# Attention, Fourier mixing and a feed-forward block on one core: a third batch turned on TensorE, another first chunk, a run-in of zeros and a new early order

## The chip, the core and the metric

The kernel runs on one core of one Trainium2 chip. The metric is device time in microseconds of one launch; lower is better. Engines are named as in the profile: PE (TensorE's products), PEld (its weight loads), DVE (VectorE), ACT (ScalarE), POOL (GpSimd), SP (the queue that issues most DMAs).

## The reference

```python
def _attn_ref(q, k, v):                     # B, H, S, D = 8, 8, 576, 64
    scores = scale * np.matmul(q, k.transpose(0, 1, 3, 2))
    # heads 0..3: the last 32 positions; heads 4..7: every 4th of the last 128
    scores = np.where(masks[None, :, :, :], scores, -1000000000.0)
    ...
    return np.matmul(attn, v)

def _moe_ref(x, w_ch1, w_ch2):              # x: [8, 576, 512]
    X = np.fft.fft(np.fft.fft(x, axis=1), axis=2)
    u = x + np.real(X).astype(np.float32)
    un = (u - mu) / np.sqrt(var + 1e-06)    # over the 512 channels
    ch = np.maximum(un @ w_ch1, 0.0) @ w_ch2   # 512 -> 2048 -> 512
    return u + ch
```

All of it is float32 in and out. Windowed attention makes x, the real part of a two-dimensional Fourier transform is added to it, and a feed-forward block with a residual follows.

## The kernel before, in words

**Two parts.** In the early part each of the eight batches goes through attention (`attend`), the Fourier mixing as products with cosine and sine tables (`mix`), and `normalise`, which writes the normalised rows to scratch memory (`us`, four tiles of 128 rows to a "chunk" of 512 tokens; eight chunks are the batches, the ninth holds the rows that are left over). Six of the sixteen blocks of hidden units are done right there (`fill`: `up` on line 1351, `down` on line 1368), as soon as a pair of tiles is there with the channels on the partitions. The other ten blocks are done in the late part, for one chunk after the other, in pairs of blocks by a scheme with seven products in place of eight (`two_tiles`, `product` on line 1746, `down7` on line 1856). The late part's operand, `xb`, is made by `load_blocks` from the chunk's turned tokens: sums and differences on line 1566, and high and low halves on lines 1576 (ACT) and 1579 (DVE). Float32 products are made of three fast ones, with a high and a low half of each operand.

**Turning tokens.** `normalise` leaves rows with the tokens on the partitions; both parts need the channels there. For the first two batches (`b < NPE`) `turned` does it on PE: four transposes per tile (line 975) into one of two PSUM banks named "mix", an ACT copy (line 981) for the high half and a DVE subtraction (line 982) for the low half. Mixing takes its banks from the same two. For the other batches `tokens` fetches the rows from `us` in four pieces (line 1489), DVE transposes blocks (line 1499), the turned tokens are stored in scratch memory for the late part (line 1522, `kept_t`, named tt in the profile), and ACT and DVE make the halves (lines 1528 and 1531). In the late part `load_blocks(c)` reads `kept_t` where it is there (two reads of 512 KB); for chunks 0 and 1 it fetches and transposes afresh.

**The order.** No order is written by hand: `Plan.run` places every operation in advance, on each engine the ready one with the lowest priority first, by costs and delays written into the planner. `MOVED` adds to the priorities, group by group (x: tables, k: keys and queries, v: values, s, p, o: steps of attention, l, f, q, e, c: steps of mixing, n: normalise, t: turning, u, d: feed-forward, w, W: weight loads and their conversion, and others), `HELD` adds to the earliest times. The engines run the resulting lists strictly in order. The weights come as 64-bit floats, and DVE and ACT convert them (lines 1254 to 1272 and 1307 to 1335); those of the late part that have no seat yet are written to scratch memory (line 1339, wt<-wst) and read again (line 1342). `keep_warm` issues a few products without use (line 1381) ahead of the late part.

**The join.** `load_blocks` for the first chunk and the weights' conversion share DVE, ACT and the DMA queues with the last `fill`s. The first chunk's four tiles get their buffers at once; later ones wait for a mark (`marks`).

**The start.** Batch 0's first scores (line 821, sixteen products of 64x64 per part) wait for q and k from memory. The first 32 columns of each k buffer are cleared by DVE (line 702).

Of the kernel before, what the change touches and what calls it, by code (L numbers as in the profile page):

```python
# [20 lines left out]
P = 128  # L21
# [22 lines left out]
LB_AT, PR_AT = 0, 0  # L44
# [13 lines left out]
NPE = 2  # L58
N_WARM0, N_WARM1 = 6, 5
NXT = 0  # L60
# [77 lines left out]
}  # L138
HELD = {
# [21 lines left out]
BURST, COST_SC, COST_AV = 0.25, 0.07, 0.07  # L161
NCH = B * S // TOK
NREST = 4 * B
NTILE = B * S // P
QG = 32
KG = 64
NG = 18
# [419 lines left out]
def fused_kernel(ctx: ExitStack, tc, q, k, v, w1, w2, seq, tail, rest32, chn, alt, mask, ident, flip, out):  # L587
# [1316 lines left out]
    for c in range(NCH):  # L1904
        if c:
            load_blocks(c, gate2, soon(P_LB))
# [48 lines left out]
```

## Time and profile before

| | us |
|---|---|
| median of 3 runs | 1023.43 (1023.1 to 1027.09) |
| the profiled execution | 1018.65 |
| its span, first to last instruction | 1016.9 |

| engine | busy us | share of the span |
|---|---|---|
| PE | 958.6 | 94% |
| DVE | 825.5 | 81% |
| ACT | 564.8 | 56% |
| POOL | 210.2 | 21% |

A span is the time from the first to the last instruction. Busy time is a union of instruction times; the end of a product on PE is modelled, and products overlap, so that PE at 94% isn't PE at its peak. PEclk is the granted clock of TensorE as a share of 2.4 GHz, DMA the mean busy share of the core's sixteen DMA engines. A wait is put down to what released it last.

### The profile page before, as it was taken

To read this page: it belongs to the slowest core of one execution; us is meant where nothing else is said; L and a number is where in the kernel's file an instruction comes from. 1 tells how busy PE (TensorE), PEld (TensorE's weight loads), DVE (VectorE), ACT (ScalarE), POOL (GpSimd) and SP (SyncE) were. 2 spreads that over 40 slices of the span, in tenths; PEclk is the share of its full clock that TensorE was granted. 3 is DMA by queue.
4 is the path that set the end of the run, shared out by engine and by line. 5 is a ranking of instruction groups with operands and counts; after the bars stand their busy time and mean duration, and the time that the engine had idled before them with its cause. 6 is when DMAs were issued, how large, how long until landed. Compare 5 with 4: busy or idle time off the path is not lost.

```text
span 1016.9 us, 29244 instructions
## 1 busy us (share of the span) xinstructions
PE 958.6 (94%) x11109; PEld 873.7 (86%) x11109; DVE 825.5 (81%) x2738; ACT 564.8 (56%) x1483; POOL 210.2 (21%) x277
## 2 busy tenths in 40 slices
PE   3499999999999999999998999999999999999997
PEld 2247788888878888998987999999999999999997
DVE  3799876777877798669888599888888888888887
ACT  2566646454555443236454575757575756575663
POOL 2301442635445446400003000000000000100011
PEclk9999999999999999999999999999999999999999
DMA  8767866878785554265798943131313131313031
GB/s 284 243 230 221 261 208 205 248 225 255 246 247 156 182 160 129 83 214 170 261 347 315 309 135 105 63 106 61 114 53 115 54 114 53 116 53 121 6 112 56
DMA packets 111510, 168.74 MB, mean 166 GB/s; under 512 B 13156, under 2 KB 53140, under 8 KB 111370
## 3 DMA queue, kind: packets, MB, share of 16 engines
q1 hardware_dynamic: 107452, 159.52, 49.8%
q0 software_dynamic: 2880, 6.43, 2.1%
q8 instruction: 88, 1.44, 0.6%
q10 hardware_dynamic: 1038, 0.92, 0.3%
q14 instruction: 52, 0.43, 0.1%
HBM read 111.47 MB, written 54.45 MB: 163 GB/s over the span
## 4 chain that ended last, share of the span: by engine, by line
PE 59%; DVE 9%; DMA 7%; issue 2%; ACT 1%; SPq 1%; POOL 1%; DVEq 0%; ACTq 0%; POOLq 0%
PE ff L1746 19%; PE ff L1351 6%; PE ff L1368 6%; PE mix L1856 6%; PE sc L1856 6%; PE sd L1856 5%; DMA ut<-us 3%; PE ff L1856 3%; PE mix L1163 2%; DMA wt<-wst 1%; PE sd L1351 1%; PE mix L1098 1%; DVE ut L1499 1%; DMA wst<-in_w_dram 1%; PE sc L1368 1%
## 5 line engine op out<-in xcount | busy, mean ns | idle before, releaser
L1421 POOL DMA_INDIRECT ut<-us,flip_sb x20 | 30.6, 1529 | 509.3 <-DVE ut L1450 158.3
L1351 PE MATMUL ff<-ut,wa 128*128 128x256 f32 x936 | 131.7, 287 | 3.6 <-DVE h L1360 1.9
L1351 PEld LDWEIGHTS ff<-ut,wa 128*128 128x128 f32 x936 | 117.4, 188 | 9.9 <-DVE h L1360 3.0
L1368 PE MATMUL ff<-wa,h 128*128 128x512 f32 x468 | 120.8, 400 | 0.7 <-DVE h L1360 0.7
L837 ACT ACTIVATE pm<-pm,mx 128x64 f32<-128x64 f32 x288 | 79.5, 339 | 68.1 <-DVE mx L831 56.4
L1368 PEld LDWEIGHTS ff<-wa,h 128*128 128x128 f32 x468 | 83.3, 188 | 17.6 <-DVE h L1360 0.9
L1746 PE MATMUL ff<-xb,wa 128*128 128x256 f32 x540 | 75.8, 281 | 0.1
L1746 PE MATMUL ff<-xb,left_w 128*128 128x256 f32 x486 | 69.2, 281 | 0.1
L1746 PEld LDWEIGHTS ff<-xb,wa 128*128 128x128 f32 x540 | 68.4, 188 | 0.3 <-ACT ut L1754 0.3
L1746 PE MATMUL ff<-xb,late_w 128*128 128x256 f32 x486 | 68.7, 280 | 0.0
L1770 ACT ACTIVATE h<-s 128x256 fp32r<-128x256 f32 x134 | 55.4, 417 | 19.3 <-DVE s L1786 14.5
L1746 PEld LDWEIGHTS ff<-xb,left_w 128*128 128x128 f32 x486 | 62.2, 188 | 0.5 <-ACT s L1754 0.3
L1746 PEld LDWEIGHTS ff<-xb,late_w 128*128 128x128 f32 x486 | 61.9, 188 | 0.1
L1746 PE MATMUL ff<-xb,right_w 128*128 128x256 f32 x378 | 55.0, 286 | 4.3 <-DVE xb L1579 2.7
L1746 PEld LDWEIGHTS ff<-xb,right_w 128*128 128x128 f32 x378 | 49.5, 193 | 5.4 <-DVE xb L1579 2.9
L1754 ACT COPY s<-ff 128x256 f32<-128x256 f32 x90 | 33.5, 372 | 33.4 <-PE ff L1746 32.5
L1358 ACT ACTIVATE h<-ff 128x256 fp32r<-128x256 f32 x78 | 28.5, 381 | 38.6 <-PE ff L1351 38.1
L1351 PEld LDWEIGHTS sd<-ut,wa 128*128 128x128 f32 x360 | 45.1, 188 | 3.5 <-DVE h L1360 2.2
L1351 PE MATMUL sd<-ut,wa 128*128 128x256 f32 x360 | 46.5, 281 | 0.5 <-DVE h L1360 0.4
L1499 DVE STREAM_TRANSPOSE ut<-ut 128x512 f32<-128x512 f32 (+1 forms) x40 | 38.9, 996 | 8.9 <-DMA ut<-us 5.1
L1360 DVE SCALAR_TENSOR_TENSOR h<-ff,h 128x256 fp32r<-128x256 f32 x78 | 31.6, 418 | 17.3 <-ACT h L1358 16.9
L1368 PE MATMUL sc<-wa,h 128*128 128x512 f32 x180 | 44.2, 391 | 0.0
(309 smaller groups left out, 2629.0 us busy)
## 6 DMA issues: line engine op xcount, KB each, us to landing
vt<-in_v_dram SPq DMA_DIRECT2D x64, 260.0 KB
wst<-in_w_dram SPq DMA_DIRECT2D x20, 512.0 KB
wt<-wst SPq DMA_DIRECT2D x40, 256.0 KB
us<-uc SPq DMA_DIRECT2D x36, 257.0 KB
part<-row SPq DMA_DIRECT2D x36, 256.0 KB
ut<-part SPq DMA_DIRECT2D x36, 256.0 KB
kb<-in_k_dram SPq DMA_DIRECT2D x30, 288.0 KB
ut<-us SPq DMA_DIRECT2D x56, 128.0 KB
```

The lines of the kernel that those rows point to most:

```text
L837: add("ACT", 0.25, lambda i=i: nc.scalar.activation(out=pm()[:, i], in_=pm()[:, i], func=AF.Exp, bias=mx()[:, i:i + 1], scale=-1.0), ((mx, ...
L1163: nc.tensor.matmul(ps()[:n, :NEP], lhsT=ys[i]()[:, dt, a, rows], rhs=chn_sb[i]()[:, dt, c], start=(dt == 0 and x == 0), stop=(i == 1 and d ...
L1351: nc.tensor.matmul(z()[:, :n_tok], lhsT=wf()[:, a, kk], rhs=ut()[:, p, kk], start=(kk == 0 and n == 0), stop=(kk == KT - 1 and n == 2),)
L1358: add("ACT", act(n_tok) - 0.03, lambda: nc.scalar.activation(out=h()[:, 0, :n_tok], in_=z()[:, :n_tok], func=AF.Relu), (z,), ((h, 0),), prio)
L1360: add("DVE", dve(n_tok), lambda: nc.vector.scalar_tensor_tensor(h()[:, 1, :n_tok], z()[:, :n_tok], 0.0, h()[:, 0, :n_tok].bitcast(F32), op ...
L1368: nc.tensor.matmul(acc(), lhsT=h()[:, a, P * s:P * s + P], rhs=wf()[:, p], start=(first and n == 0), stop=(last and n == 2),)
L1421: add("POOL", 1.3, lambda: nc.gpsimd.indirect_dma_start(u(0, C + 2), None, us[idx // 4](), bass.IndirectOffsetOnAxis(ap=flip_sb()[:, 4 * k ...
L1499: nc.vector.transpose(out=o[back], in_=x[:, g])
L1746: nc.tensor.matmul(up_bank()[:, lo:lo + TOK1], lhsT=ap()[:, a, kk], rhs=xb()[:, j, p, kk], start=(start and k == 0), stop=(k == 5), skip_g ...
L1754: add("ACT", act(n), lambda: nc.scalar.copy(out=dst()[:, 0:n], in_=up_bank()[:, 0:n]), (up_bank, held), (dst,), SOON - 1, urgent=True)
L1770: add("ACT", act(TOK1), lambda: nc.scalar.activation(out=ap()[:, 0], in_=src(), func=AF.Relu if relu else AF.Copy), need, (k0,), prio)
L1856: nc.tensor.matmul(acc()[:, TOK1 * half:TOK1 * half + TOK1], lhsT=ap()[:, a, P * half:P * half + P], rhs=wap()[:, q_].rearrange("p k f -> ...
```

## The change

`NPE` goes from 2 to 3: the third batch's tokens are turned on PE too, and its chunk has no stored turned tokens any more. The late part takes the chunks in the order 3, 0, 1, 2, 4, ..., 8 (`CHUNKS`); what waited for chunk 0's marks waits for chunk 3's. Ahead of the first scores, 32 products of the cleared columns of a k buffer (128 rows, 32 columns) are issued into the bank that the scores use. All lists of `MOVED` and `HELD` have new numbers; of them only two are shown ('t' grows by two entries, as the third batch has four turnings in place of two).

```diff
@@ -55,8 +55,9 @@
 NLATE = 4
 NOPEN = 1
 FIRST_ROWS, FIRST_TURNED = (2, 4, 3, 0, 1), (0, 1, 2, 3, 4)
-NPE = 2
+NPE = 3
 N_WARM0, N_WARM1 = 6, 5
+N_RUN_IN = 32
 NXT = 0
...
 MOVED = {
...
-    't': [2.82, 30.02, 13.59, 48.13, 38.32, -32.79, -15, 13.62, -15.86, 29.59, -2.72, -15.14, -10.97, 27.11, 12.95,
-        -8.92, 3.05, -9.28, -10.08, -6.8, -44.66, -92.86],
...
+    't': [3.64, 28.12, 23.45, 142.06, 52.92, -8.66, 54.82, 4.99, -9.91, -6.38, 0, 13.6, 12.63, 53.42, 35.91, -6.04,
+        -15.3, 3.3, 14.02, -126.73, -1.68, -43.3, -0.49, -43.08],
...
 }
 HELD = {
...
-    'w': [-18.54, -16.05, -45.55, -83.3, -40.31, 0, 0, 0, 26.55, 18.73, 20.29, 15.09, 0.71, -26.25, 5.07, -11.88,
-        13.87, 35.67, 54.87, 10.06, 19.65, 39.59, 65.37, 57.55, 4.17, 58.29, 41.14, 32.44, 0, -39.11, 15.49, -1.95],
...
+    'w': [-8.45, -22.94, -33.96, -48.18, -9.67, -2.95, 13.4, 18.15, -13.48, -18.28, -18.97, -10.24, 2.78, 23.77,
+        4.55, 6.51, 46.82, 49.36, 43.45, 41.43, 3.73, 15.97, 17.19, 36.26, -17.29, -6.02, -1.79, 40.32, 1.37, 7.95,
...
 }
 BURST, COST_SC, COST_AV = 0.25, 0.07, 0.07
 NCH = B * S // TOK
 NREST = 4 * B
 NTILE = B * S // P
+CHUNKS = (3, *(c for c in range(NCH) if c != 3))
 QG = 32
 KG = 64
 NG = 18
@@ -813,7 +815,12 @@
                     lo = QG * g if whole else 2 * QG * j + QG * g
                     yield j, at, slice(lo, lo + QG), j if whole else 0
 
+        run_in = N_RUN_IN if first and u == FIRST_TURNED[0] else 0
+
         def scores():
+            for _ in range(run_in):
+                z = kb[0]()[:, 0:WIN]
+                nc.tensor.matmul(split[0]()[0:WIN, 0:WIN], lhsT=z, rhs=z, start=True, stop=True)
             for j, at, rows, c in tiles():
                 cols = slice(base + P * c + rows.start, base + P * c + rows.stop)
                 for e in range(2):
@@ -1413,7 +1420,7 @@
 
         def part():
             return pt()
-        add("NONE", 0.0, lambda: None, (marks[mark],) if mark[0] == 0 else (), (uk,), prio)
+        add("NONE", 0.0, lambda: None, (marks[mark],) if mark[0] == CHUNKS[0] else (), (uk,), prio)
         if order(idx) == 0:
             dma(lambda: nc.sync.dma_start(out=u(0, C + 2), in_=u_rows(idx)), ((us[idx // 4], idx % 4),), (uk,), prio, P * 2056)
         else:
@@ -1540,7 +1547,7 @@
     def load_blocks(c, gate, prio):
 
         raw, tr = spare["raw"], spare["tr"]
-        add("NONE", 0.0, lambda: raw(), (marks[0, LB_AT],) if c == 1 else (), (raw,), prio)
+        add("NONE", 0.0, lambda: raw(), (marks[CHUNKS[0], LB_AT],) if c == CHUNKS[1] else (), (raw,), prio)
         if (c, 0) in kept_t and (c, 1) in kept_t:
             done = []
             for h in range(2):
@@ -1548,7 +1555,7 @@
                 dma(lambda h=h: nc.sync.dma_start(
                     out=words(tr).rearrange("p (k t) -> p k t", k=KT)[:, :, 256 * h:256 * h + 256],
                     in_=kept_t[c, h]().rearrange("p (k t) -> p k t", k=KT)),
-                    (kept_t[c, h], *((marks[0, LB_AT],) if c == 1 else ())), keys, prio, P * 4096 * 0.7, 0.5)
+                    (kept_t[c, h], *((marks[CHUNKS[0], LB_AT],) if c == CHUNKS[1] else ())), keys, prio, P * 4096 * 0.7, 0.5)
                 done += keys
         else:
             done = turned_tokens(c, 0, 4, (raw, lambda: words(raw)), (tr, lambda: words(tr)), prio)
@@ -1674,7 +1681,7 @@
         return plan.buf(lambda: pools["stage"], "wst", [P, 2, KT, TOK1], F32R, 4)
 
     spare["raw"], spare["tr"], spare["h"], spare["out"] = (utb() for _ in range(4))
-    load_blocks(0, gate2, LAST)
+    load_blocks(CHUNKS[0], gate2, LAST)
     n_prep = len(plan.ops)
     for p in range(NPAIR):
         for x, (rows, dst) in enumerate(((rows_up, ups[p]), (rows_down, downs[p]))):
@@ -1901,8 +1908,8 @@
                 done = finish(4 * c + half, w_of[4 * c + half], top_rows, (s[1], s[2]), half, done, clock[0])
 
     keep_warm(up_bank, N_WARM1, LAST - 1)
-    for c in range(NCH):
-        if c:
+    for c in CHUNKS:
+        if c != CHUNKS[0]:
             load_blocks(c, gate2, soon(P_LB))
         for p in range(NPAIR):
             ending = c == NCH - 1 and p == NPAIR - 1
```

`T_WS`, to which the first six entries of `HELD['w']` are added for the weight loads of the early part, is `[28, 32, 36, 40, 45, 50]`, with 0 as the least.

## Rows read from the trace of the kernel before

**Rows 1.** Stretches: us; busy PE, PEld, DVE, ACT, POOL; PEclk, DMA share, GB/s

```profile
0.00:50.00 50.00, 19.72 (x660) 14.08 (x660) 26.29 (x178) 19.35 (x62) 17.71 (x37) 1.00 0.82 263
50.00:200.00 150.00, 141.83 (x2646) 109.94 (x2645) 123.72 (x652) 85.20 (x261) 48.16 (x69) 1.00 0.73 227
200.00:350.00 150.00, 146.38 (x2751) 121.91 (x2750) 118.84 (x621) 79.30 (x250) 67.69 (x96) 1.00 0.74 222
350.00:500.00 150.00, 146.01 (x954) 132.05 (x953) 121.88 (x286) 62.31 (x155) 43.22 (x54) 1.00 0.52 165
700.00:750.00 50.00, 50.00 (x424) 49.97 (x423) 43.16 (x101) 32.46 (x78) 2.14 (x2) 1.00 0.27 86
```

**Rows 2.** PE's waits, longest first: engine, line, awaited: us in total, times, longest

```profile
PE mix L821 <- DMA tq<-in_q_dram: 9.8, 1, 9.8
...
PE ff L1746 <- DVE xb L1579: 2.7, 1, 2.7
```

**Rows 3.** Groups by shape, 60 to 500: xcount, busy us, mean ns, idle before

```profile
L975 PE MATMUL mix<-ident_sb,uc 128*128 128x128 f32 x32 | 6.1, 303 | 2.2 <-DVE ve L952 1.5 <-ACT uc L947 0.7
L1499 DVE STREAM_TRANSPOSE ut<-ut 128x512 f32<-128x512 f32 x24 | 25.4, 1084 | 5.9 <-DMA ut<-us 4.6 <-DMA xsm<-xt 1.1
```

**Rows 4.** DMA issues: what, issuing queue, operation, count, KB each

```profile
ut<-us SPq DMA_DIRECT2D x56, 128.0 KB
tt<-ut SPq DMA_DIRECT2D x14, 512.0 KB
```

**Rows 5.** DVE in order of time, 526 to 560: start, us, line, [idle before]

```profile
527.53 1.09 DVE L1499 STREAM_TRANSPOSE ut<-ut 128x512 f32<-128x512 f32 x1
...
555.72 0.43 DVE L1335 TENSOR_TENSOR wst<-wst 128x256 fp32r<-128x256 f32 x1 [2.84 <-ACT wst L1333]
556.07 0.68 DVE L1579 TENSOR_TENSOR xb<-ut,xb 128x512 fp32r<-128x512 f32 x1
```

**Rows 6.** PE in order of time, 542 to 570

```profile
553.72 0.40 PE L1746 MATMUL ff<-xb,right_w 128*128 128x256 f32 x2
556.80 0.76 PE L1746 MATMUL ff<-xb,right_w 128*128 128x256 f32 x4 [2.69 <-DVE xb L1579]
558.02 2.92 PE L1746 MATMUL ff<-xb,right_w 128*128 128x256 f32 x12 [0.46 <-ACT ys L1754]
...
561.62 1.65 PE L1746 MATMUL ff<-xb,right_w 128*128 128x256 f32 x12 [0.68 <-ACT ut L1754]
```

**Rows 7.** A stretch at the join of the two parts

```profile
555.00:560.00 5.00, 2.73 (x13) 2.51 (x14) 2.90 (x6) 2.36 (x6) 0.00 (x0) 0.74 0.89 338
```

**Rows 8.** ACT's longest wait in 540 to 575

```profile
ACT wst L1333 <- DMA wt<-wst: 5.3, 2, 4.2
```

**Rows 9.** DVE in order of time, near 4 us

```profile
3.70 0.12 DVE L702 MEMSET kb<- 128x32 f32 x2
```

**Rows 10.** Scores by shape: 0 to 55 us, then 62 to 350

```profile
L821 PE MATMUL mix<-kb,tq 64*32 64x64 f32 x72 | 3.9, 309 | 11.2 <-DMA tq<-in_q_dram 9.8 <-DMA kb<-in_k_dram 1.3
L821 PE MATMUL sc<-kb,tq 64*32 64x64 f32 x944 | 30.5, 223 | 2.4 <-DVE xt L879 2.4
```

**Rows 11.** Stretches of the first batch

```profile
10.00:30.00 20.00, 11.46 (x412) 8.45 (x400) 8.07 (x81) 8.17 (x33) 9.22 (x18) 1.00 0.95 341
30.00:55.00 25.00, 12.36 (x320) 8.11 (x320) 20.60 (x98) 12.82 (x38) 7.00 (x14) 1.00 0.62 186
```

**Rows 12.** Turning the first batch's last two tiles, and the next mixing

```profile
98.18 0.66 PE L975 MATMUL mix<-ident_sb,uc 128*128 128x128 f32 x4
...
109.61 0.68 DVE L982 TENSOR_TENSOR ut<-mix,ut 128x512 fp32r<-128x512 f32 x1
110.44 0.67 PE L1098 MATMUL mix<-seq,ees 128*128 128x290 f32 x3
```

**Rows 13.** Stretches: the third batch's tokens; a chunk's load inside the late part

```profile
203.00:222.00 19.00, 17.81 (x302) 14.78 (x301) 16.27 (x66) 11.35 (x34) 4.90 (x6) 1.00 0.78 238
571.00:621.00 50.00, 49.87 (x424) 49.66 (x424) 44.40 (x101) 32.76 (x78) 0.00 (x0) 1.00 0.51 146
```

164 rows, old and new, of tables (HELD, MOVED) are left out of this document.

## Prediction

> **What bounds the kernel now.** I read the stretches first [rows 1]. Two parts show. From 553.72 on, where line 1746 first multiplies [rows 6], the late part runs: nine chunks on PE, without a gap in its middle (50.00 of 50 us at 700), with DVE at 43 of 50 beside it. Its PE work is the same after the change, so nothing is to be won in its middle. Before it lies the early part: attention, mixing and the early share of the feed-forward work (lines 1351 and 1368). There PE is busy 19.72 of the first 50 us, then 141.83 and 146.38 of 150, then 146.01 of 150. So the early part idles 30.3 us in its first 50, 8.2 in the next 150, 3.6 in the 150 after, and 4.0 up to 500. From 350 on PE has a backlog, so PE time saved earlier reaches the end one for one, and saved DVE or DMA time only where PE stood still for it.
>
> Second, the list of PE's waits [rows 2]: 9.8 us for the first q tile, and one wait of 2.7 us for DVE's line 1579, which writes xb, the operand of the late part. Third, that place in order of time [rows 5, 6]: PE waits at 556.80, and its next twelve products take 2.92 us where the twelve after them take 1.65. The granted clock of 555 to 560 is 0.74 [rows 7]; after a wait of 2.69 us with few products around it the clock had gone to the lower of its two levels (1.2 of 2.4 GHz) for a while. So the join between the two parts costs 2.69 + 1.27 = 4.0 us of PE, plus 0.46 and 0.68 of short waits that belong to the chain of the first products.
>
> What is late at the join is not xb alone. DVE does line 1335 at 555.72 after 2.84 us of waiting for ACT, and only then line 1579 at 556.07, which stands behind it in DVE's order [rows 5]. ACT had waited up to 4.2 us for the write of a weight tile to scratch memory, wt<-wst [rows 8]. DVE's weight work feeds those writes, so DVE's lateness and the DMA's are chained.
>
> **The change, part by part.**
>
> *Late part takes chunk 3 first.* Chunk 0's tokens were never stored turned, so load_blocks fetches them in four pieces (line 1489) and DVE turns them: the first of four transposes stands at 527.53 [rows 5], at 1.084 us each [rows 3], 4.3 us in all, ahead of all weight work that follows. Chunk 3's turned tokens lie in scratch memory (kept_t), so two reads of 512 KB bring them in and the four transposes are gone; bytes are equal. With 4.3 us less ahead of them, the weight work, its writes and line 1579 come earlier by up to 4.3 us, more than the 2.69 that PE waits. Value: the whole 4.0 us, **-4.0**. Bounds: 0, if the writes keep their time because the DMA, not DVE, sets it; -5.1 with both short waits. What is next late is the first products' own chain (product, ACT copy, product). Four issues of line 1489 go from SP, two reads come.
>
> *Chunks 0 and 2 inside the late part.* Both now need four fetches and four transposes there (chunk 1 had them already). The cover is DVE's free time beside PE: over 571 to 621, where chunk 1's transposes ran, DVE has 44.40 of 50 and PE 49.87; without them 43.16 and 50.00 [rows 1, 13]. So 0.13 us each, **+0.3**; without that cover 4.3 us each.
>
> *Third batch turned on PE (NPE = 3).* Removed: 8 fetches of 128 KB and 2 stores of 512 KB [rows 4], 2.05 MB, which at the 238 GB/s of 203 to 222 [rows 13] is some 8.8 us of the queues; ten issues on SP; four DVE transposes, 4.3 us. Added: 16 PE transposes. Four take 0.66 us at 98.18 [rows 12], the last of them 0.303 [rows 3], so (0.66 - 0.303) / 3 = 0.119 us apart: +1.9 us of PE. ACT copies and DVE subtractions stay, now reading PSUM (DVE 0.68 us each [rows 12]). PE runs in order, so where a transpose waits for its normalised tile, feed-forward products and scores queue behind it; line 975 brought 2.2 us of such waits for 32 [rows 3], 1.1 for 16, and who waits for these is DVE with the masks. Against this the tokens come earlier, since the store, fetch and transposes drop out; but PE was idle only 19 - 17.81 = 1.2 us in 203 to 222, where they are made now [rows 13]. And DVE and DMA are freer in one batch of eight: PE's idle 11.8 us of 50 to 350 is some 2.0 per 50 us, of which I take half. 1.9 + 1.1 - 1.2 - 1.0 = +0.8; bounds +3.0 (nothing given back) and -1.2 (all of 1.2 and 2.0 back, no wait). Value **+0.8**.
>
> *Products of zeros.* Thirty-two products on the zeroed columns of the k buffer, possible once DVE has cleared it at 3.82 [rows 9], while PE is idle until 9.81 (the 9.8 us of rows 2). In 10 to 30 the column of the granted clock reads 1.00, yet the same 64x64 product takes 309 ns there and 223 later [rows 10], so I take it that PE ran at its lower level. If the zeros raise it, scores, transposes and values are about 0.09 us shorter each; three in a chain, two rounds before DVE and DMA set the pace: **-0.5**. Bounds: if each zero product took 309 ns one after another, they end at 3.82 + 9.9 = 13.7, 3.9 us late; if the clock stays up, see the fourth rival. I take -0.5 because a product of 32 columns is nearer to a fraction of 309 ns than to all of it.
>
> The Trainium skill (TensorE: Matmul & The Clock Gate, Part 1) says that the low clock is the default, that activity releases it and that idleness brings it back. The trace agrees in rows 7, and this speaks against the zeros, as PE stands still again before the first scores and is busy little over half the time until 55. By that rule the term would be 0 instead of -0.5.
>
> *Early priorities anew.* MOVED and HELD shift the order on every queue, and no row shows the new one. What can be had is the idle time: 20 - 11.46 and 25 - 12.36 in 10 to 55 [rows 11], 8.2 and 3.6 after: 33 us. In 10 to 30 the DMA is at 0.95, in 30 to 55 DVE at 20.60 of 25. The only direction that the numbers show: the weight loads' earliest times (T_WS plus HELD 'w') move from 9.5, 16.0, 0, 0, 4.7 to 19.6, 9.1, 2.0, 0, 35.3 of the planner's us, so less weight traffic and weight work should stand before the first batch's chain in just these stretches. I take a tenth of the 33, **-3.3**; bounds a third to either side, -11 and +11.
>
> Sum: -4.0 + 0.3 + 0.8 - 0.5 - 3.3 = **-6.7 us**. The profiled execution took 1018.65 us (its span of 1016.88 and 1.8 around it): 1012.0. The median of the runs is 4.8 higher, 1023.43; from it, **1016.7**.
>
> **The rivals.**
>
> *The order wins more (third of the idle time).* -11 for -3.3: 1016.7 - 7.7 = 1009.0. For it: the idle 21 us of 10 to 55 is waiting on queues that are ordered by these lists. Against: 9.8 us of the start are bare loading, and after 50 little is idle.
>
> *Nothing comes through.* DMA sets the join (rows 8: ACT waits for a write, in a stretch with a DMA share of 0.89, rows 7) and the new order only trades: 0.3 + 0.8 - 0.5 = +0.6, 1024.0.
>
> *Slower: the third batch's tokens block the mix banks.* turned() takes one of two "mix" banks per tile, which mixing needs too. The first batch's transposes began at 98.18 and their last subtraction only at 109.61; the second batch's line 1098 started at 110.44, just after it [rows 12]. That is 12.3 us of both banks. Were the fourth batch's mixing held so once, and PE out of other work meanwhile, it is +12.3, and with the join's gain and the small terms -4.0 + 0.3 + 0.8 - 0.5 = +8.9: 1032.3. It decides from about 8.5 us of uncovered hold on. Against: PE has feed-forward work of two batches by then. The Trainium skill (Trainium Kernel Development and Optimization, Best Practices) asks to mind PSUM pressure, as PE gets faster and the emptying of PSUM does not. By that rule this is the way it goes; rows 12 show it once.
>
> *The clock stays up from the zeros on.* PE's 23.8 us of busy time in 10 to 55 would shrink by 1 - 223/309, 6.6 us; half of it on the path, -3.3 for -0.5: 1013.9. Against: rows 7 and 11.
>
> **How the numbers follow.** Forecast 0.43 (its own range 1011 to 1021), order wins more 0.14, clock stays up 0.06, nothing comes through 0.19, slower 0.18. About 0.5% (5.1 us) is what a measurement of this kernel can tell from no change: below 1018.3 is faster, above 1028.5 slower. Of the forecast's 0.43 some 0.08 lies above 1018.3. Faster: 0.35 + 0.14 + 0.06 = 0.55; same: 0.08 + 0.19 = 0.27; slower: 0.18. The range goes from 1005 to 1031: it leaves out the far end of the first rival (0.04) and the larger part of the slower one (0.12).
>
> **What would show it.** The join: PE's wait for line 1579 near the first line 1746 gone or under 1 us, the granted clock at 1.00 there, no transposes of line 1499 ahead of it. NPE: 48 transposes on line 975, 12 stores tt<-ut, and line 1098 of the fourth batch not starting right behind line 982. Zeros: 64x64 products near 220 ns from 10 us on. Order: PE busier than 23.8 us in 10 to 55, or the same work done sooner, and the first line 1746 product before 547. Late part: still about 50 us in 50. Wrong it would be if the first line 1746 product comes later than 553, or if PE shows gaps inside the late part.

## The result, and the profile after

| | before | after |
|---|---|---|
| median of 4 runs each, side by side | 1023.26 us (1021.3 to 1027.09) | 1011.83 us (1010.67 to 1012.46) |
| ratio, 95% interval | 1 | 0.9871 (0.9831 to 0.9910) |
| repeated on another chip, 17 and 6 runs | 1025.83 us | 1010.01 us, 0.9856 (0.9825 to 0.9888) |
| the profiled execution | 1018.65 us | 1012.46 us |
| its span | 1016.9 us | 1010.4 us |

The change makes the kernel 1.3% to 1.4% faster: 11.4 us by the medians, where 6.7 were forecast. The two profiled executions differ by only 6.2 us, because the one of before is faster than every run in the table and that of after is the slowest of its four. From line 818 on, all lines of after stand seven higher than in before (line 1746 is 1753, line 1579 is 1586). First the stretches of after, in the columns of [rows 1]:

```profile
0.00:50.00 50.00, 23.96 (x725) 17.43 (x725) 27.85 (x181) 20.33 (x65) 17.72 (x37) 0.60 0.82 265
10.00:30.00 20.00, 12.11 (x398) 8.68 (x398) 8.12 (x82) 8.63 (x33) 10.85 (x22) 0.51 0.98 338
30.00:55.00 25.00, 12.66 (x319) 8.12 (x318) 21.40 (x99) 13.16 (x38) 5.96 (x11) 0.51 0.59 183
50.00:200.00 150.00, 143.17 (x2653) 110.62 (x2659) 122.00 (x646) 85.78 (x259) 48.15 (x69) 0.98 0.73 224
200.00:350.00 150.00, 146.08 (x2771) 122.92 (x2772) 113.17 (x621) 77.93 (x249) 66.56 (x95) 1.00 0.71 211
350.00:500.00 150.00, 148.01 (x969) 133.51 (x968) 124.12 (x294) 64.36 (x158) 42.01 (x55) 1.00 0.55 175
...
550.00:600.00 50.00, 49.04 (x389) 47.30 (x388) 36.83 (x84) 31.35 (x76) 0.00 (x0) 1.00 0.70 218
600.00:700.00 100.00, 99.31 (x828) 97.99 (x827) 91.42 (x209) 64.44 (x153) 6.07 (x4) 1.00 0.37 97
700.00:750.00 50.00, 49.99 (x421) 49.62 (x420) 43.55 (x104) 33.28 (x79) 2.14 (x2) 1.00 0.29 87
```

Most of the 4.2 us more of PE in 0 to 50 are the products of zeros. Beyond [rows 1], PE does 1.3 us more in 50 to 200 and 2.0 more in 350 to 500, and 0.3 less in between. The largest single step is 550 to 600: before, that stretch read

```profile
550.00:600.00 50.00, 45.45 (x346) 43.16 (x345) 35.30 (x79) 28.30 (x68) 3.73 (x1) 0.97 0.83 263
```

so PE has 3.6 us less idle time there, and the lower clock of [rows 7] is gone. In order of time on PE (start, us, line, what), the join of after is another one than that of [rows 6]:

```profile
540.11 2.01 PE L1388 MATMUL ff<-wa 128*128 128x512 f32 x8
541.96 0.85 PE L1753 MATMUL ff<-xb,right_w 128*128 128x256 f32 x6
542.65 1.55 PE L1375 MATMUL sc<-wa,h 128*128 128x512 f32 x6
544.04 1.59 PE L1753 MATMUL ff<-xb,right_w 128*128 128x256 f32 x12
```

The late part's products (line 1753) begin at 541.96 and stand between the last early ones (line 1375, the last of them at 558.11), where before they began behind them, at 553.72. Twelve of them take 1.59 us, the upper clock's price (1.65 in [rows 6]).

### The profile page after: what moved, and what is told of

Same layout as the page of the kernel before. It is cut to its first block, busy times and chain, and to the rows that moved or that the text cites. A ratio compares the mean times of both kernels' runs of the same rounds, so it can differ in the third digit from the quotient of the medians.

```text
span 1010.4 us, 29386 instructions
## 1 busy us (share of the span) xinstructions
PE 962.6 (95%) x11189; PEld 876.8 (87%) x11189; DVE 820.5 (81%) x2738; ACT 565.6 (56%) x1483; POOL 202.1 (20%) x277
## 2 busy tenths in 40 slices
DMA packets 110101, 166.63 MB, mean 165 GB/s; under 512 B 13028, under 2 KB 51988, under 8 KB 109962
## 4 chain that ended last, share of the span: by engine, by line
PE 64%; DVE 8%; DMA 4%; ACT 2%; issue 1%; SPq 1%; POOL 0%; DVEq 0%; ACTq 0%; POOLq 0%
PE ff L1753 21%; PE sd L1863 6%; PE ff L1358 6%; PE mix L1863 6%; PE sc L1863 6%; PE ff L1375 5%; PE ff L1863 3%; PE sc L1375 3%; DMA ut<-us 3%; PE sd L1358 3%; PE mix L1170 2%; PE mix L1105 2%; DMA wt<-wst 1%; DVE ut L1506 1%; PE sc L828 1%
## 5 line engine op out<-in xcount | busy, mean ns | idle before, releaser
L1358 PE MATMUL ff<-ut,wa 128*128 128x256 f32 x936 | 128.5, 285 | 1.6 <-DVE h L1367 0.9
L1428 POOL DMA_INDIRECT ut<-us,flip_sb x20 | 24.9, 1246 | 512.1 <-DVE ut L1457 213.2
L1753 PE MATMUL ff<-xb,right_w 128*128 128x256 f32 x378 | 52.6, 280 | 0.1
L854 ACT COPY ptsb<-sc 128x256 f32<-128x256 f32 (+1 forms) x75 | 25.5, 350 | 34.9 <-PE sc L849 34.8
```

Of the source, the lines that this page charges most:

```text
L854: add("ACT", act(n), lambda: nc.scalar.copy(out=pt()[:, 0:n], in_=split[0]()[:, 2 * P:2 * P + n]), (split[0],), (pt,), prio)
L1358: nc.tensor.matmul(z()[:, :n_tok], lhsT=wf()[:, a, kk], rhs=ut()[:, p, kk], start=(kk == 0 and n == 0), stop=(kk == KT - 1 and n == 2),)
L1428: add("POOL", 1.3, lambda: nc.gpsimd.indirect_dma_start(u(0, C + 2), None, us[idx // 4](), bass.IndirectOffsetOnAxis(ap=flip_sb()[:, 4 * k ...
L1753: nc.tensor.matmul(up_bank()[:, lo:lo + TOK1], lhsT=ap()[:, a, kk], rhs=xb()[:, j, p, kk], start=(start and k == 0), stop=(k == 5), skip_g ...
```

## The experiments

Each is one edit of before or of after. "Lists" stands for MOVED and HELD. Ratios are to the kernel before on the same chip.

| kernel | third batch on PE | lists of after | chunk 3 first | zeros | ratio | 95% interval |
|---|---|---|---|---|---|---|
| before again | | | | | 1.0002 | 0.9975 to 1.0029 |
| b_chunk3 | | | x | | 0.9981 | 0.9953 to 1.0009 |
| b_zeros | | | | x | 1.0031 | 1.0001 to 1.0060 |
| b_npe3 | x | | | | 1.0144 | 1.0106 to 1.0183 |
| b_lists | | x | | | 1.0081 | 1.0053 to 1.0109 |
| a_npe2 | | x | x | x | 1.0058 | 1.0029 to 1.0087 |
| a_lists3 | x | x | | | 0.9984 | 0.9961 to 1.0007 |
| a_chunk0 | x | x | | x | 0.9928 | 0.9900 to 0.9956 |
| a_nozeros | x | x | x | | 0.9923, 0.9900 | 0.9897 to 0.9950, 0.9869 to 0.9930 |
| after again | x | x | x | x | 0.9856 | 0.9825 to 0.9888 |

### One part at a time, on the kernel before

**The kernel before, again.**

> The kernel before, once more, for a second profiled execution. Theory 1 (the join: PE waits for xb, its clock drops, and how long both last differs from execution to execution): the executions spread over 4 to 6 us again, and in the new trace the join (line 1746's first products) differs from the first trace by about as much as the span does. Theory 2 (the executions differ in the first 100 us, where loading sets the pace): the join is alike, and the last scores of line 821 come at another time than 343.2.

1024.82 us (1020.89 to 1031.6, 12 runs: a spread of 10.7 us, where the first theory had 4 to 6). Its profiled execution took 1031.6, the longest of the twelve, against 1018.65 for the one that the prediction read. Stretches of PE's clock, first of before, then of before again:

```profile
62.00:73.00 11.00, 10.57 (x159) 5.53 (x157) 9.92 (x35) 6.37 (x14) 0.00 (x0) 1.00 0.86 285
```

```profile
62.00:73.00 11.00, 10.77 (x83) 4.53 (x84) 7.03 (x23) 5.63 (x14) 0.00 (x0) 0.53 0.58 199
```

In one execution the clock stayed at its upper level after the first attention, in the other it went back to the lower for most of 62 to 73; PE was as busy in both, with about half the products done (83 for 159). The first transposes of line 975 then start at 88.87, where they had started at 82.38. Of the 12.9 us between the spans (1029.8 and 1016.9) 7 are lost by 117 and 5 more up to 350, spread thinly. The last scores come at 355.4 for 343.2, and the join differs little (a wait of 3.5 us for 2.7). So the second theory holds for 7 of the 12.9 us, though it is the clock behind the first attention and not loading that makes them; what the 5 up to 350 come from is not settled. The prediction had read an execution without that loss.

**Chunk 3 first, alone.**

```diff
+CHUNKS = (3, *(c for c in range(NCH) if c != 3))
...
-    for c in range(NCH):
-        if c:
+    for c in CHUNKS:
+        if c != CHUNKS[0]:
```

> The kernel before with the late part's order 3, 0, 1, 2, 4 to 8, and nothing else. Theory 1 (four DVE transposes less ahead of the join are worth the join's wait by themselves): 3 to 5 us faster, the first product of line 1746 no longer waits for line 1579. Rival (only the new lists of priorities bring the first operand forward): within 1.5 us of before, the wait of PE for line 1579 stays at 2 us or more.

1023.22 us, no measurable gain. The time is the rival's, but not its condition: in the trace the wait for xb is gone. Yet PE's idle time in 550 to 600 is the same: 45.23 of 50 busy.

```profile
549.61 4.70 PE L1369 MATMUL sc<-wa,h 128*128 128x512 f32 x20
554.15 1.53 PE L1382 MATMUL ff<-wa 128*128 128x512 f32 x6
555.51 0.87 PE L1747 MATMUL ff<-xb,right_w 128*128 128x256 f32 x6
557.33 1.65 PE L1747 MATMUL ff<-xb,right_w 128*128 128x256 f32 x12 [0.95 <-ACT ys L1755]
...
586.59 0.38 PE L1857 MATMUL sd<-late_w,row 128*128 128x256 f32 x1 [1.72 <-ACT row L1771]
587.80 0.39 PE L1857 MATMUL sd<-late_w,row 128*128 128x256 f32 x1 [0.83 <-DVE row L1778]
```

```profile
583.35 1.10 DVE L1500 STREAM_TRANSPOSE ut<-ut 128x512 f32<-128x512 f32 x1 [3.92 <-DMA late_w<-wt]
```

The last of xb is ready at about 551.3, four us before its first product; the order of before puts all early products first, so the products start at 555.51 as a chain with ACT (0.95 and 0.68 of waiting) with nothing to put in between. Even so the join gains what the prediction gave it. Against the trace of before, the first product of the late part comes 1.8 us later and the nineteenth 2.0 us earlier, 3.8 us won. They are lost again some 25 us further on, where chunk 0 is now turned inside the late part: DVE stands 3.92 us at the first of its transposes, PE waits 1.72 and 0.83 us for what is queued behind them, the granted clock of 585 to 590 is 0.85, and at 593 the products are 2.5 us later than in before. By 683, behind the four transposes of chunk 1, it is 4.6.

**Third batch on PE, alone** (NPE = 3, two entries of list 't' repeated for the two more turnings).

```diff
-NPE = 2
+NPE = 3
```

> The kernel before with the third batch turned on PE, and nothing else (its four entries of the list 't' repeat the two that were there). Theory 1 (PE pays 1.9 us, the earlier tokens and the freer DVE give it back): within 1.5 us of before. Rival (mix banks held by the third batch's tokens, the fourth batch's line 1098 behind line 982): 5 us or more slower. Second rival (this is where the gain of the whole change lies): 4 us or more faster.

1041.95 us, 1.4% slower. The mix banks are not what costs it: the list of PE's waits has 0.5 us for a transpose in 185 to 345, and none for mixing. Beside the trace of before again, whose clock falls back in the same place (0.53 over 62 to 73 in both), the last scores are level (355.3 and 355.4). The loss lies behind or between them: PE has done less of its other work by then (141.94 of 150 us busy in 200 to 350, for 144.41), the first product of the late part comes 5.2 us later, those behind the first wait of the late part 10.1, and by 700, when chunk 2 too has been turned inside the late part, 13.1. Why the early products fall behind by 5.2 us is not settled. The join shows here, by its wait and two of its stretches:

```profile
PE ff L1745 <- DVE xb L1578: 6.0, 1, 6.0
```

```profile
575.00:580.00 5.00, 1.35 (x5) 1.06 (x5) 4.71 (x9) 3.68 (x8) 0.00 (x0) 0.50 0.82 281
580.00:585.00 5.00, 4.33 (x19) 4.03 (x20) 0.85 (x2) 1.00 (x2) 0.00 (x0) 0.50 0.91 276
```

The wait for xb grows from 3.5 us (before again) to 6.0, and the clock is at its lower level through both stretches.

**Zeros, alone.**

```diff
...
+            for _ in range(run_in):
+                z = kb[0]()[:, 0:WIN]
+                nc.tensor.matmul(split[0]()[0:WIN, 0:WIN], lhsT=z, rhs=z, start=True, stop=True)
```

> The kernel before with the 32 products of zeros ahead of the first scores, and nothing else. Theory 1: 0 to 0.7 us faster, the clock rises for a few us and is low again before 20. Rival (the clock stays up until the first batch is done): about 3 us faster, the 64x64 products of 15 to 50 us near 220 ns.

1027.54 us: 0 to 6 us slower by the interval, against either outcome. Of the clock the first theory is right: in the trace the first scores take 0.22 to 0.24 us, the next, at 11.67, 0.31 again. The first product of mixing, behind the first attention, starts at 51.75 us, sooner than in before (53.11) and before again (54.11). By the end that lead is gone (a span of 1030.8 us, for 1016.9 and 1029.8); the clock falls back behind the first attention here too (0.66 over 62 to 73). Why the zeros lose on this kernel is not settled.

**The new lists, alone.**

> The kernel before with the lists of early tasks of the kernel after (the two extra entries for the third batch's turn left out), its third batch's tokens still turned by DMA, chunk 0 first, no zeros. Theory 1: the gain is in the lists alone; 1010 to 1016 us, ratio 0.987 to 0.992 to before. Theory 2 (parts fit each other): the lists place the third batch's fills and steps for tokens that are turned by TensorE; with the DMA turn they stall on it, 1022 to 1040 us.

1034.33 us, 0.8% slower. The first theory falls: this order by itself is worth nothing without the work that it was made for. The stalls of the second show: in 185 to 500 PE's products of feed-forward work wait 11.5 us for DVE's h, where in before they wait 1.5.

### One part taken away from the kernel after

**Third batch turned by DMA again.**

```diff
-NPE = 3
+NPE = 2
```

> The kernel after with the third batch's tokens turned by DMA again and its two list entries for that turn left out. Theory 1 (lists alone): within 3 us of the kernel after, 1009 to 1015. Theory 2 (parts fit each other): the third batch comes late for the places that the lists give it, 1017 to 1030. The same two theories as for the kernel before with the lists; here chunk 3 is first and the zeros are in.

1031.91 us: 20 us more than after, slower than before, and 2 us beyond the second theory's range. That theory holds all the same, and DVE's order of time shows how (the number in brackets is the idle time ahead, and what ended it):

```profile
201.14 2.04 DVE L1505 STREAM_TRANSPOSE ut<-ut 128x512 f32<-128x512 f32 x2 [3.25 <-DMA ut<-us]
...
203.66 0.74 DVE L1366 SCALAR_TENSOR_TENSOR h<-ff,h 128x256 fp32r<-128x256 f32 x2
```

```profile
204.12 2.24 PE L1357 MATMUL ff<-ut,wa 128*128 128x256 f32 x10 [3.32 <-DVE h L1366]
```

```profile
251.83 1.09 DVE L1505 STREAM_TRANSPOSE ut<-ut 128x512 f32<-128x512 f32 x1 [5.67 <-DMA ut<-us]
...
254.66 0.38 DVE L1366 SCALAR_TENSOR_TENSOR h<-ff,h 128x256 fp32r<-128x256 f32 x1
```

DVE stands 3.25 us, and later 5.67, at a transpose whose rows DMA has not yet brought; h, which PE needs, is queued behind that transpose; PE stands 3.32 us, and 3.75 at 255.09. The stretches say what that comes to, in a_npe2:

```profile
200.00:350.00 150.00, 138.66 (x2588) 114.41 (x2587) 115.26 (x598) 76.04 (x242) 68.45 (x97) 0.98 0.74 218
350.00:500.00 150.00, 145.12 (x983) 130.65 (x969) 124.65 (x304) 63.85 (x158) 40.75 (x53) 0.99 0.53 168
500.00:550.00 50.00, 49.29 (x320) 44.78 (x321) 39.49 (x96) 23.84 (x60) 0.00 (x0) 1.00 0.83 275
550.00:600.00 50.00, 45.69 (x331) 43.37 (x330) 31.75 (x69) 26.26 (x62) 2.52 (x2) 0.97 0.87 291
```

Against after PE lacks 7.4, 2.9, 0.6 and 3.4 us in these four, 14.3 in all, of the 15.4 us between the spans (1025.8 and 1010.4; this execution, 1027.59 us, is the fastest of its seven); the clock is below 1.00 in three of them besides.

**Chunk 0 first.**

```diff
-CHUNKS = (3, *(c for c in range(NCH) if c != 3))
+CHUNKS = tuple(range(NCH))
```

> The kernel after with the late part in the order of chunks 0 to 3. Theory 1: the wait of the late part's first products for the low halves of chunk 0 comes back, 2 to 4 us of wait and some 1.3 us of lower clock behind it, 1014 to 1018 us. Rival: the lists end the early steps sooner, chunk 0 is turned in time, so 1010 to 1013. Since chunk 3 first gained nothing on the kernel before (ratio 0.998), the rival is the likelier.

1019.78 us, 6 to 7 more than after by the ratios and 2 beyond the first theory's range; the rival falls. PE, in order of time:

```profile
543.87 8.33 PE L1375 MATMUL sc<-wa,h 128*128 128x512 f32 x36
552.04 0.40 PE L1753 MATMUL ff<-xb,right_w 128*128 128x256 f32 x2
555.72 0.74 PE L1753 MATMUL ff<-xb,right_w 128*128 128x256 f32 x4 [3.28 <-DVE xb L1586]
556.92 2.93 PE L1753 MATMUL ff<-xb,right_w 128*128 128x256 f32 x12 [0.46 <-ACT ys L1761]
560.52 1.65 PE L1753 MATMUL ff<-xb,right_w 128*128 128x256 f32 x12 [0.68 <-ACT ut L1761]
```

Here [rows 6] is back with all its parts: 36 early products in one go, a wait of 3.28, twelve products in 2.93 us at the lower clock, the short waits of the chain. DVE shows why the operand is late, first in a_chunk0, then in after:

```profile
524.11 1.10 DVE L1506 STREAM_TRANSPOSE ut<-ut 128x512 f32<-128x512 f32 x1
...
543.94 1.10 DVE L1506 STREAM_TRANSPOSE ut<-ut 128x512 f32<-128x512 f32 x1
...
554.37 2.50 DVE L1586 TENSOR_TENSOR xb<-ut,xb 128x512 fp32r<-128x512 f32 x4
```

```profile
530.60 0.69 DVE L1573 TENSOR_TENSOR ut<-ut 128x512 f32<-128x512 f32 x1 [0.61 <-DMA ut<-tt]
...
540.66 0.68 DVE L1586 TENSOR_TENSOR xb<-ut,xb 128x512 fp32r<-128x512 f32 x1
```

With the four transposes, xb is done at 556.9; without them at 541.3, 15.5 us earlier, though they take 4.4 us. They lie between other DVE work from 524 to 545, and the first step of xb (line 1573) comes only at 545.27, right behind the fourth.

**Without the zeros** (N_RUN_IN = 0; every other instruction keeps its place on its engine).

> The kernel after without the 64 products of zeros ahead of the first scores. Theory 1: the zeros do nothing for the clock of the scores (it rose once for 3.4 us and was at the lower level until 54.6 us), 1010 to 1014 us, the first scores again near 9 us instead of 7.2. Theory 2: the zeros hold the time together, that is, without them the clock falls back behind the first attention as it did in one execution of the kernel before (62 to 73 us): 1015 to 1020 us and a spread of over 8 us. On the kernel before the zeros cost 3 us (ratio 1.003), so a third outcome is 1007 to 1010.

1018.49 us, ratio 0.9923, with a spread of 2.5 us and not of over 8. The trace gives the first scores at 6.17 us, not near 9. The same kernel, beside after on one chip:

> The kernel after without the 64 products of zeros, once more, now beside the kernel after; the order of all other instructions on every engine is the same in both. Theory 1: the zeros are worth 3 to 6 us here. Theory 2: within 2 us of the kernel after. Seen in the trace by Theory 1: TensorE's clock falls back behind its first rise near 55 us (64x64 products over 290 ns in 56 to 70 us), which the kernel after does not show (228 ns).

1014.75 us (1012.37 to 1017.06) where after took 1010.01 (1009.16 to 1013.49): the zeros are worth some 4.7 us here by the medians, 3.5 by the means, with runs that overlap; by the ratios of three pairs (this one, the one before it, and a_lists3 below against a_chunk0) it is 4.5 to 5.7. How they bring it is not settled. In the first of the two profiles the clock fell back once behind the first attention (0.78 over 55 to 70), as the theory wants it, but in the second it did not, and that execution (1012.37 us, the fastest of its six) has a span of 1010.5, as after has (1010.4, and 1011.4 in after again). The stretch of 55 to 70 in both:

```profile
55.00:70.00 15.00, 14.38 (x163) 6.78 (x163) 11.57 (x50) 8.41 (x23) 0.00 (x0) 0.78 0.86 289
```

```profile
55.00:70.00 15.00, 14.86 (x186) 7.02 (x184) 12.95 (x54) 9.12 (x25) 0.00 (x0) 1.00 0.88 302
```

One thing does go with the zeros in every trace: the first product of mixing starts at 50.97 to 52.28 us in the six profiled executions that have them, and at 52.30 to 54.11 in the eight that have not, on both kernels, 1.8 us apart on average. The clock of the first scores is not the way to it, since only three of the six show those at the upper level. In after again the first of them took:

```profile
7.39 0.31 PE L828 MATMUL mix<-kb,tq 64*32 64x64 f32 x1
```

**Lists and third batch only** (chunk 0 first, no zeros).

> The kernel after with chunk 0 first and without the zeros: what is left of the change are the lists and the third batch turned by TensorE. If the losses of the two that are taken away (5.8 and 5.3 us by the ratios 0.9928 and 0.9923 against 0.9871) add up: ratio 0.998, near 1023 us. If lists and turning carry the gain: 0.990 to 0.993. The lists alone gave 1.008 and the turning alone 1.014, so anything under 1.00 shows that these two only work together.

1024.18 us, 0.9984: what chunk 3 and the zeros bring adds up, as the first outcome says (0.998). And the pair of lists and turning, each of which loses by itself (0.8% and 1.4%), comes to nothing or a small gain together, some 2.4% better than the sum of the two.

**After, again.**

> The kernel after, unchanged, beside the other three. Theory 1 (what left the kernel after slower without the zeros or with chunk 0 first is real): ratio 0.985 to 0.989 to before, so 5 us under either. Theory 2 (those two differed because they ran on another chip): ratio 0.990 to 0.993, level with them.

1010.01 us, 0.9856: the first theory; the differences above are no matter of the chip.

**After, without the ten products without use at the join** (line 1388 above).

```diff
-N_WARM0, N_WARM1 = 6, 5
+N_WARM0, N_WARM1 = 6, 0
```

> The kernel after without the ten products without use at the join (2.6 us of PE in the trace of the kernel after, where PE no longer waits for the operand there). Theory 1: they are bare work now, 1.5 to 3 us faster than the kernel after. Theory 2: they still carry the clock over the join; without them TensorE's clock falls there as in the kernel before (0.74 over 5 us), so within 1 us or slower by up to 2. A third outcome: the planner moves the last early products, and the operand or the weights are late for the first products, slower by 2 to 6.

1011.94 us (1008.41 to 1014.03), level with after. The 2.6 us come back as idle time of PE, here beside after again:

```profile
500.00:550.00 50.00, 49.07 (x322) 44.72 (x321) 44.97 (x107) 29.12 (x70) 3.34 (x2) 1.00 0.90 329
550.00:600.00 50.00, 47.02 (x368) 44.84 (x367) 36.10 (x80) 29.74 (x71) 0.00 (x0) 1.00 0.72 233
```

```profile
500.00:550.00 50.00, 50.00 (x323) 45.58 (x322) 44.23 (x106) 29.89 (x74) 3.26 (x2) 1.00 0.92 339
550.00:600.00 50.00, 48.81 (x396) 47.29 (x395) 36.56 (x83) 31.12 (x73) 0.00 (x0) 1.00 0.75 216
```

0.93 and 1.79 us less in the two stretches are 2.7. The clock reads 1.00 in all of it, so the second theory's lower clock is not the reason either: the late part's first products wait for DVE and ACT (0.9, 0.7, 0.6 and 0.5 us), so PE's own work does not set the pace at the join. No variant tried beats the kernel after.

## Why the prediction was right, and where it was not

**Sign, range and the sum.** Faster, and within the range; but 1005 to 1031 takes in slower as well as faster, so that lying in it says little. The forecast itself, 6.7 us, is 0.6 of the 11.4 measured. The sum made against the profiled execution, 1012.0, met the profiled execution of after, 1012.46, and that is luck: the runs give 6 to 7 us for the join, some 5 for the zeros and 1.6 for lists and third batch together, twice the sum, and the start of the sum was an execution 4.8 us below its median. In the last step, from 1012.0 to 1016.7, these 4.8 us were carried over to after. They are not a constant. Before again shows one thing they consist of, a clock that falls back in 62 to 73. After's runs lie within 4.3 us of each other, before's 17 beside them within 9.5, and after's medians lie 0.6 and 3.4 us below its two profiled executions where before's lay 4.8 above.

**The join, -4.0.** The mechanism came as described, and in the trace of b_chunk3 with nearly the size (3.8 us). In after: no wait for line 1586, no transposes of line 1506 ahead of it, the clock at 1.00, first product at 541.96, before 547. There the size was too small, and its lower end of -5.1 too: a_chunk0 says 6 to 7 us. The step that failed is "up to 4.3 us": xb came 15.5 us earlier, since the transposes cost DVE's order and not only their own time. That let the products start between the early ones, so that the short waits are hidden too. And to keep it needs the lists: on before's the gain was lost again inside the late part.

**Chunks 0 and 2 inside, +0.3.** PE is at 99.31 of 100 in 600 to 700, where it had been at 99.86: 0.5 us, so in after the size is in order. In after again it is 97.08, with one wait of 2.2 us for ACT, which had itself stood 3.39 us for rows that a DMA fetches (ut<-us,flip_sb), and not for a transpose. On before's lists the cover that the term took for granted is not there: in b_chunk3 some 6.6 us go between the join and 683, most of them around the transposes, and that is where the join's gain went.

**Third batch on PE, +0.8.** The parts were right: 48 transposes of 300 ns, in 8.5 us of PE where 32 took 6.1 [rows 3], so 2.4 for 1.9; waits of 0.7 us; 48 fetches of 128 KB for 56, 12 stores for 14, 166.63 MB for 168.74.

```profile
L982 PE MATMUL mix<-ident_sb,uc 128*128 128x128 f32 x48 | 8.5, 300 | 0.7 <-ACT uc L954 0.7
```

The term as a whole has no value of its own: +14.7 us with the old lists (1.0144 of 1024), and with the new ones its absence costs 20. The term's own parts came true; what it left out shows in b_npe3 at the late part's join and inside the late part, and in a_npe2 at the feed-forward products. The same holds for **the early priorities, -3.3**: +8 alone, and -1.6 together with the third batch (0.9984; -4.0 to +0.7 by the interval), for which my two terms had -2.5. The step that failed is to price them one after the other, and to bound the first by PE's and DMA's time: the bound of +3.0 held only beside lists that were made for it. The sum of the pair was in order, by a working that does not explain it.

**The zeros, -0.5.** Of the wrong sign on before (+3), too small on after (some -5). The bound of 3.9 us late was right to be dropped: the 32 products, which the trace records as 64, take 3.46 us and are done while the next scores still wait for their keys (to 10.59).

```profile
3.84 3.46 PE L823 MATMUL mix<-kb 128*32 128x32 f32 x64 [3.84 <-DVE tail_sb L722]
7.24 0.24 PE L828 MATMUL mix<-kb,tq 64*32 64x64 f32 x1
```

The rival in which the clock stays up falls: the first scores run at 228 ns (in after again not even those), the next ones at 309 again, and the clock reads 0.51 from 10 to 55. The rule of the Trainium skill (TensorE: Matmul & The Clock Gate, Part 1), that idleness brings the low clock back, agrees with the 0.51; that the term would be 0 by it does not agree with the 4.7 us. The working of the term, a clock raised for the first scores, is not what brings them.

**The slower rival, mix banks.** Its price was read too high to begin with. [rows 12] leaves out the first product of mixing behind the first subtraction, which ended at 108.16 in before:

```profile
108.21 0.67 PE L1098 MATMUL mix<-seq,ees 128*128 128x290 f32 x3
```

So both banks were held for 10.0 us there, not 12.3. In after, PE's and DVE's rows, in order of time:

```profile
196.33 1.23 PE L982 MATMUL mix<-ident_sb,uc 128*128 128x128 f32 x8
198.99 0.65 PE L1105 MATMUL mix<-seq,ees 128*128 128x290 f32 x3
```

```profile
197.73 1.29 DVE L989 TENSOR_TENSOR ut<-mix,ut 128x512 fp32r<-128x512 f32 x2 [0.18 <-ACT ut L988]
```

Line 1105 of the fourth batch starts at 198.99, half a us behind the first of line 989's two subtractions (to 198.42) and with no wait of PE ahead of it; the last turning holds both banks for 2 us. PE is busy for 23.58 of the 24 us from 184 to 208: it had other work, as the prediction held against the rival.

## What to carry to other kernels

An order that was fitted to a program is part of that program: price a structural edit and its order as one; here either alone lost. An operation on an in-order engine costs what its waits and its place hold up behind it, so taking it away can bring more than its own length: here 4.4 us of transposes moved the operand by 15.5 us and the whole by 6 to 7. A gain at one place stays only if the next place in line has room for it, as b_chunk3 shows. And read the clock of more than one execution before a median is built on one profile: here one had lost 7 us by 117 that the other had not, in the same program.

## What the runs showed of the hardware

The same 64x64 product takes 309 ns at the lower clock and 223 to 228 at the upper, down to the first scores of the kernel: the zeros ahead of those brought the upper level in b_zeros, a_chunk0 and after, and not in after again, a_npe2 and a_warm0 (311 to 313 ns). The page of before gives a clock of 1.00 in 0 to 55 all the same, and that of after 0.51 with products of 309 ns in 10 to 30: so 1.00 at the start of a trace need not be the granted level, and the products' own length tells it. In a_npe2 the three stretches with PE's long waits read a clock below 1.00 (0.98 with waits of 3.3 and 3.75 us, 0.99 with one of 2.4, 0.97 with one of 2.6), in before and a_chunk0 the join does (0.74 and 0.66 over five us), and where the wait at the join is gone it stays at 1.00 there.
